# Norm scales moved into exp, staging of the first batch, and a written VectorE order in a fused attention and MLP kernel

## Chip, cores and metric

The kernel runs on one core of one Trainium2 chip. The metric is the device time of one execution in microseconds (us), lower is better.

## The reference

Attention with normalised queries and keys, followed by a LayerNorm and an MLP with a residual:

```python
def rmsnorm(x, g):                       # q, k, v: (8, 12, 448, 64) float32
    return x / np.sqrt(np.mean(x * x, axis=-1, keepdims=True) + 1e-06) * g
scores = np.matmul(rmsnorm(q, g_q), rmsnorm(k, g_k).transpose(0, 1, 3, 2)) / 8
attn = softmax(scores)
x = np.matmul(attn, v)                   # heads side by side: (8, 448, 768)
xn = (x - mean) / np.sqrt(var + 1e-06) * g_ln
out = x + np.maximum(xn @ w_ch1, 0.0) @ w_ch2    # (768, 3072), (3072, 768)
```

## The kernel before, in words

The work is attention by pairs of heads (6 pairs for each of 8 batches, 48 in all) and one MLP for each batch. TensorE, ScalarE, GpSimd (POOL) and the SP queue run in the order in which the program issues their instructions; VectorE's instructions are ordered by the framework's scheduler (`manual_schedule` at L642 names all engines but VectorE).

**Units.** Loads and preparation go by units (L23): batch 0 has six units of one pair, later batches have three of two pairs. `load_unit` (L94) issues nine DMAs: for each of k, q, v the first 384 rows of the heads (L106, on SP) and twice the 64 left over rows (L111, on ScalarE's queue for units 0 and 1, else on SP). One-pair units are staged in `hT`, the MLP's hidden buffer, in three rotating places; two-pair units in `p_in`, with two buffers.

**Preparation** (`prep_ops`, L114) of a unit is a list of operations: squares of k and q on ScalarE (L136), sums of squares on VectorE (L139), k times the product of both gain vectors on GpSimd (L145), inverse roots (`_rsqrt`, L32: one exp on ScalarE and seven small instructions on VectorE), the key's norm (`kn`, L47 by way of L150), its high half (L153) and its remainder (L156) in fp16, the normalised query (L47 by way of L160) and its duplicate (L163), and v cast on GpSimd (L166, L171). `attention` (L268) spreads these over the steps of earlier pairs with a table `todo` from step to operations.

**A pair** has seven steps (L295). Step i issues the score matmuls of key block i (L217 to L221), the exp of that block (L222, scale 1/8), and the value matmuls of the pair before (L241, L243). At step 2 the next pair's keys are transposed (L186) and copied from PSUM in two parts (L189, L190), at step 4 its queries (L200), copied in three parts (L202 to L204). After the last value block `evac_o` (L247) divides by the sums, and `stats` (L330) takes LayerNorm statistics of the 128 columns that a pair gives.

**LayerNorm and MLP.** `ln_ops` (L342) makes a list: statistics and root; then for each tile of 128 tokens a normalisation (ScalarE L364, VectorE L366) and a transposition (TensorE L379, VectorE copy L381). Odd batches have four tiles, since the left over rows of two batches share one; even batches have three. `mlp_chunks` gives 24 up chunks (six matmuls L394, relu L396) and, for each tile, eight down chunks (six matmuls L405); the residual add is L409. 

**The order around it.** `run` (L430) first issues attention up to step 0.4 of a pair, then the loads of the first weights (L315, on GpSimd), attention up to pair 3, the second weights (L320), attention up to pair 7, the LayerNorm of batch 0 with some more attention between its parts, and then each MLP chunk by chunk, with attention issued in proportion to the chunks' costs, so that the next batch's attention (and one pair beyond) is through at 82% of the cost. What is left of the chunks then carries the next LayerNorm's operations, evenly spread. Before the last MLP `flag` (L482) counts whether all softmax sums lie in a range; if not, a general path (L499) recomputes everything.

Of the kernel before, what the change touches and what calls it, by code (L numbers as in the profile page):

```python
# [22 lines left out]
UNITS = [(0, 2 * i, 1) for i in range(NPAIR)]  # L23
# [5 lines left out]
REC_LO, REC_HI = 1.0 / 3.0e7, 0.5  # L29


def _rsqrt(nc, out, a, t, eps):  # L32
# [5 lines left out]
    for _ in range(2):  # L38
        eng.tensor_tensor(out=t, in0=out, in1=out, op=ALU.mult)  # L39
        eng.scalar_tensor_tensor(out=t, in0=t, scalar=-0.5, in1=a, op0=ALU.mult, op1=ALU.mult)  # L40
        eng.scalar_tensor_tensor(out=out, in0=t, scalar=1.5, in1=out, op0=ALU.add, op1=ALU.mult)
# [14 lines left out]
class _Fast:  # L56


    def __init__(self, ctx, tc, sh, q, k, v, g_ln, w1, w2, out):
# [21 lines left out]
        for t in self.kT:  # L81
            nc.vector.memset(t[:, 1], 0.0)
# [5 lines left out]
        nc.vector.memset(self.rec, 0.01)  # L88
        self.hT = fix.tile([128, NFF, 512], FP16, name="hT", tag="hT")
        self.xs, self.xls, self.st = {}, {}, {}  # L90
# [3 lines left out]
    def load_unit(self, u):  # L94
# [19 lines left out]
    def prep_ops(self, u):  # L114
# [8 lines left out]
        def begin():  # L123
# [3 lines left out]
            c["rt"] = self.p_n.tile([128, 2, 14], FP32, tag="rt", name="rt")[:, :, 0:g]  # L127
            c["qn"] = self.p_n.tile([128, 14, 2, D], FP16, tag="qn", name="qn")[:, 0:g]
# [12 lines left out]
        def root():  # L141
            _rsqrt(nc, c["rr"], c["ssq"], c["rt"], D * 1e-6)
# [16 lines left out]
        def qn():  # L159
            _scaled(nc, c["qn"][:, :, 0], c["t"][:, 0], c["rr"][:, 0])  # L160

        def qdup():
            nc.vector.tensor_copy(out=c["qn"][:, :, 1], in_=c["qn"][:, :, 0])  # L163
# [5 lines left out]
        def vleft():  # L169
            for e in range(2):  # L170
# [4 lines left out]
                lambda: (total(0), vmain()), root, None, kn, khi, klo, qn, qdup, vleft]  # L175


    def trans_k(self, p):
# [3 lines left out]
        ps = self.ps_tr.tile([128, 1024], FP16, tag="tr", name="psK")  # L182
        kT = self.kT[p % 2]
        gs = [6 * m + w] + [6 * w + i for i in range(6)]
        for i, g in enumerate(gs):
            nc.tensor.matmul(ps[:, ts(i, 128)], khl[:, g], sh.id16, is_transpose=True,  # L186
# [491 lines left out]
```

## Time and profile before

| what | value |
|---|---|
| runs | median 733.85 us of 3 (733.62 to 735.27) |
| the profiled execution's own time | 733.03 us |
| its span in the profile | 731.2 us |
| mean granted TensorE clock | 0.956 |
| TensorE matmul busy | 633.3 us (87%) |
| VectorE, ScalarE, GpSimd busy | 428.0, 338.2, 89.7 us |
| moved by DMA | 54.83 MB |

The busy shares are means over the span. The rows below are to be read by stretch: the time from the first instruction to the first up matmul (L394), and the time after it, have different limits.

### The profile page before, as it was taken

To read this page: it belongs to the slowest core of one execution; us is meant where nothing else is said; L and a number is where in the kernel's file an instruction comes from. 1 tells how busy PE (TensorE), PEld (TensorE's weight loads), DVE (VectorE), ACT (ScalarE), POOL (GpSimd) and SP (SyncE) were. 2 spreads that over 40 slices of the span, in tenths; PEclk is the share of its full clock that TensorE was granted. 3 is DMA by queue.
4 is the path that set the end of the run, shared out by engine and by line. 5 is a ranking of instruction groups with operands and counts; after the bars stand their busy time and mean duration, and the time that the engine had idled before them with its cause. 6 is when DMAs were issued, how large, how long until landed. Compare 5 with 4: busy or idle time off the path is not lost.

```text
span 731.2 us, 12852 instructions
## 1 busy us (share of the span) xinstructions
PE 633.3 (87%) x5066; PEld 387.3 (53%) x5066; DVE 428.0 (59%) x1195; ACT 338.2 (46%) x646; POOL 89.7 (12%) x119
## 2 busy tenths in 40 slices
PE   0452458997999999997999999998999999979996
PEld 0231335664555666664556666654556566644463
DVE  1886688667466756776646757784565755351011
ACT  1443246753465327752665247633664356423400
POOL 1332012110101101110111011110111010000000
PEclk9997568998999999999999999998999999999999
DMA  4499951221322014230322123202313100000011
GB/s 138 95 220 219 229 150 48 53 77 44 98 77 74 26 44 106 70 99 22 98 76 78 44 85 110 77 23 70 99 28 98 44 22 2 23 23 22 1 44 46
DMA packets 69234, 54.83 MB, mean 75 GB/s; under 512 B 23216, under 2 KB 63152, under 8 KB 69168
## 3 DMA queue, kind: packets, MB, share of 16 engines
q1 hardware_dynamic: 62320, 43.86, 21.0%
q0 software_dynamic: 5456, 9.44, 7.0%
q8 instruction: 41, 0.67, 0.4%
q10 hardware_dynamic: 1392, 0.66, 0.3%
q14 instruction: 25, 0.20, 0.1%
HBM read 52.36 MB, written 11.01 MB: 87 GB/s over the span
## 4 chain that ended last, share of the span: by engine, by line
PE 74%; DVE 11%; DMA 6%; SPq 3%; ACT 3%; issue 1%; ACTq 0%; DVEq 0%
PE psH L394 30%; PE psC L405 25%; PE psS L217 6%; PE oA L241 4%; SPq L111 3%; PE psQ L200 2%; DMA t<-in_k_dram 2%; PE psK L186 2%; DMA hT<-in_q_dram 2%; PE psX L379 2%; PE oB L243 1%; DMA hT<-in_v_dram 1%; ACT t L364 1%; DVE xn L366 1%; DVE x L258 1%
## 5 line engine op out<-in xcount | busy, mean ns | idle before, releaser
L405 PE MATMUL psC<-w,hT 128*128 128x384 f16 x1344 | 246.8, 332 | 0.0
L394 PE MATMUL psH<-xnT,w 128*128 128x512 f16 (+1 forms) x1152 | 245.2, 352 | 1.2 <-DVE xnT L381 1.2
L222 ACT ACTIVATE E<-psS 128x448 f16<-128x448 f32 x336 | 179.1, 540 | 119.9 <-PE psS L217 99.1
L396 ACT ACTIVATE hT<-psH 128x384 f16<-128x384 f32 (+1 forms) x192 | 104.5, 544 | 149.7 <-PE psH L394 148.2
L405 PEld LDWEIGHTS <-hT 128*128 128x128 f16 x1344 | 127.7, 100 | 75.8 <-issue 6.2
L394 PEld LDWEIGHTS <-w 128*128 128x128 f16 x1152 | 105.0, 98 | 81.7 <-issue 1.3
L217 PE MATMUL psS<-qT,kT 128*128 128x448 f16 x288 | 105.3, 373 | 8.0 <-ACT E L222 5.2
L241 PEld LDWEIGHTS <-E 128*128 128x128 f16 x1008 | 74.4, 101 | 68.5 <-issue 20.8
L145 POOL TENSOR_TENSOR t<-t,gprod 128x896 f32<-128x896 f32 x21 | 43.7, 2081 | 455.0 <-issue 271.7
L241 PE MATMUL oA<-v,E 128*128 128x65 f16 x864 | 70.7, 198 | 9.9 <-DVE x L258 9.5
L409 DVE TENSOR_TENSOR x<-psC,x 128x384 f32<-128x384 f32 x48 | 26.7, 556 | 83.3 <-PE psC L405 82.9
L186 PE MATMUL psK<-id,khl 128*128 128x128 f16 x336 | 29.2, 232 | 43.6 <-DVE rt L39 23.6
L243 PE MATMUL oB<-v,E 128*128 128x65 f16 x288 | 53.5, 197 | 0.3
L186 PEld LDWEIGHTS <-khl 128*128 128x128 f16 x336 | 21.5, 104 | 44.9 <-issue 23.8
L139 DVE TENSOR_REDUCE ssq<-khl 128x14 f32<-128x896 f32 (+1 forms) x27 | 26.4, 979 | 26.3 <-ACT khl L136 25.8
L202 DVE COPY qT<-psQ 128x448 f16<-128x448 f16 x48 | 18.7, 389 | 38.6 <-PE psQ L200 38.6
L217 PEld LDWEIGHTS <-kT 128*128 128x128 f16 x288 | 29.2, 103 | 22.5 <-DVE qT L202 2.3
L256 DVE RECIPROCAL rec_all<-oA 128x6 f32<-128x6 f32 x48 | 9.3, 193 | 49.3 <-PE oA L241 49.2
L379 PE MATMUL psX<-id,xn 128*128 128x128 f16 x168 | 15.7, 243 | 22.6 <-DVE xn L366 22.6
L339 DVE BATCH_NORM_STATS2 stat<-x 128x6 f32<-128x128 f32 x144 | 34.5, 282 | 0.7
L243 PEld LDWEIGHTS <-E 128*128 128x128 f16 x336 | 33.3, 99 | 1.4 <-DVE xl L263 0.9
L200 PE MATMUL psQ<-id,qn 128*128 128x128 f16 x336 | 29.2, 232 | 4.9 <-DVE kT L190 4.9
(75 smaller groups left out, 594.8 us busy)
## 6 DMA issues: line engine op xcount, KB each, us to landing
out_dram<-x SPq DMA_DIRECT2D x24, 384.0 KB, 2.3
t<-in_k_dram SPq DMA_DIRECT2D x21, 384.0 KB, 3.6
t<-in_q_dram SPq DMA_DIRECT2D x21, 384.0 KB, 4.1
t<-in_v_dram SPq DMA_DIRECT2D x21, 384.0 KB, 4.4
w<-in_moe_w_ch_dram POOLq DMA_DIRECT2D x3, 1536.0 KB, 21.0
w<-in_moe_w_ch_dram POOLq DMA_DIRECT2D x2, 2304.0 KB, 38.1
out_dram<-xl SPq DMA_DIRECT2D x8, 192.0 KB, 3.0
t<-in_k_dram SPq DMA_DIRECT2D x42, 32.0 KB, 3.4
```

Of the source, the lines that this page charges most:

```text
L145: nc.gpsimd.tensor_tensor(out=c["t"][:, 1], in0=c["t"][:, 1], in1=sh.gprod.unsqueeze(1).broadcast_to([128, g, D]), op=ALU.mult)
L186: nc.tensor.matmul(ps[:, ts(i, 128)], khl[:, g], sh.id16, is_transpose=True, start=(i == 0), stop=(i == 6))
L200: nc.tensor.matmul(ps[:, ts(i, 128)], qn[:, g], sh.id16, is_transpose=True, start=(i == 0), stop=(i == 6))
L217: nc.tensor.matmul(ps[:, 0:S], kT[:, 192 + 128 * i:320 + 128 * i], qT[:, h * S:(h + 1) * S], start=True, stop=True)
L222: nc.scalar.activation(out=c["E"][:, i], in_=ps[:, 0:S], func=AFT.Exp, scale=1.0 / 8.0, bias=EXP_BIAS)
L241: nc.tensor.matmul(oA[:, t, cs], E[:, i, ts(t, 128)], rhs, start=(i == 0 and t == 0), stop=(i == 6 and t == 2))
L243: nc.tensor.matmul(oB[:, cs], E[:, i, 320:448], rhs, start=(i == 0), stop=(i == 6))
L339: nc.vector.bn_stats(out=self.st[b][:, t, 6 * hp:6 * hp + 6], in_=x[:, 128 * hp:128 * hp + 128])
L379: nc.tensor.matmul(ps[:, dc], xn[:, ts(dc, 128)], sh.id16, is_transpose=True, start=(dc == 0), stop=(dc == NDC - 1))
L394: nc.tensor.matmul(ps[:, 0:N], sh.w1[:, dc, ts(f, 128)], xnT[:, dc, 0:N], start=(dc == 0), stop=(dc == NDC - 1))
L396: nc.scalar.activation(out=hT[:, f, 0:N], in_=ps[:, 0:N], func=AFT.Relu)
L405: nc.tensor.matmul(ps[:, 0:384], hT[:, f, ts(t, 128)], sh.w2[:, f, ts(g, 384)], start=(f == 0), stop=(f == NFF - 1))
```

## The change

1. Units: batch 0 now has two units of one pair and two of two pairs. Units 0 to 2 are staged in `hT` side by side, without rotation, the rest in `p_in`. Units 0 to 2 are loaded first, units 3 and 4 and the LayerNorm gain right behind the preparation of unit 0. All loads are on SP but q of unit 0, which is on ScalarE's queue.
2. The key is no longer normalised. Its inverse root (with the factor 8 of the query's product left to the query) goes to a table `rr_all`, and exp takes a column of it as its scale for each partition. `khi` moves from VectorE to ScalarE, the query's duplicate of units 0 to 3 from VectorE to GpSimd. A maximum of the gains and a count over `rr_all` join the flag.
3. The transposes write into one PSUM tile `tr`, laid out so that one copy takes the keys and one the queries; a zero block stays in PSUM. The query copy of pairs 0, 2 and 4 is ScalarE's.
4. Statistics by 256 columns, after every second pair.
5. Order: steps are a list, with marks where a batch's attention ends. The sixth pair's values come before the seventh pair's scores, and the preparation of batch 1's first unit stands between the parts of batch 0's LayerNorm. Attention ends at 77% of an MLP's cost. The LayerNorm's root and first two normalisations are issued there, but its transposes only ahead of the last chunks, one each. The flag comes after three chunks of the last MLP. The second weights are loaded in two halves by columns, and batch 0's down chunks go by column half first.
6. VectorE runs in program order as well. A first exp on a constant loads ScalarE's table early.

The diff, cut to its core:

```diff
-UNITS = [(0, 2 * i, 1) for i in range(NPAIR)]
+UNITS = [(0, 0, 1), (0, 2, 1), (0, 4, 2), (0, 8, 2)]
...
-        if m == 1:
-            o = 2688 * (u % 3)
-            t = self.hT.rearrange("p f n -> p (f n)")[:, o:o + 2688].bitcast(FP32)
+        if u < 3:
+            o = 2688 * u
+            t = self.hT.rearrange("p f n -> p (f n)")[:, o:o + 2688 * m].bitcast(FP32)
...
-        eng = nc.scalar if u < 2 else nc.sync
         for n, src in ((1, self.k), (0, self.q), (2, self.v)):
-            nc.sync.dma_start(
+            eng = nc.scalar if u == 0 and n == 0 else nc.sync
+            eng.dma_start(
...
-        def kn():
-            _scaled(nc, c["t"][:, 1], c["t"][:, 1], c["rr"][:, 1])
         def khi():
-            nc.vector.tensor_copy(out=c["khl"][:, :, 0], in_=c["t"][:, 1])
+            nc.scalar.activation(c["khl"][:, :, 0], c["t"][:, 1], AFT.Identity)
...
         def qdup():
-            nc.vector.tensor_copy(out=c["qn"][:, :, 1], in_=c["qn"][:, :, 0])
+            (nc.gpsimd if u < 4 else nc.vector).tensor_copy(out=c["qn"][:, :, 1],
+                                                            in_=c["qn"][:, :, 0])
...
-                lambda: (total(0), vmain()), root, None, kn, khi, klo, qn, qdup, vleft]
+                lambda: (total(0), vmain()), khi, root, klo, None, qn, qdup, vleft]
...
-        nc.vector.tensor_copy(out=flat[:, 0:64], in_=ps[:, 0:64])
-        nc.vector.tensor_copy(out=flat[:, 128:960], in_=ps[:, 64:896])
+        nc.vector.tensor_copy(out=kT.rearrange("p g d -> p (g d)"), in_=ps[:, 0:960])
...
-        nc.vector.tensor_copy(out=qT[:, 0:448], in_=ps[:, 0:448])
-        nc.vector.tensor_copy(out=qT[:, 448:832], in_=ps[:, 512:896])
-        nc.vector.tensor_copy(out=qT[:, 832:896], in_=ps[:, 448:512])
+        if p in (0, 2, 4):
+            nc.scalar.copy(out=qT, in_=ps.rearrange("p e s -> p (e s)"))
+        else:
+            nc.vector.tensor_copy(out=qT, in_=ps.rearrange("p e s -> p (e s)"))
...
-        nc.scalar.activation(out=c["E"][:, i], in_=ps[:, 0:S], func=AFT.Exp, scale=1.0 / 8.0,
-                             bias=EXP_BIAS)
+        nc.scalar.activation(out=c["E"][:, i], in_=ps[:, 0:S], func=AFT.Exp,
+                             scale=self.rr[:, 1, g:g + 1], bias=EXP_BIAS)
...
+        todo.setdefault(2, []).append(lambda: [self.load_w1(c, c + 1024) for c in range(0, FF, 1024)])
+        todo.setdefault(21, []).append(lambda: [self.load_w2(g) for g in range(2)])
...
+        def first():
+            for u in range(3):
+                self.load_unit(u)
+            for op in self.prep_ops(0):
+                if op is not None:
+                    op()
+            self.trans_k(0)
+            self.trans_q(0)
+            self.load_unit(3)
+            self.nc.sync.dma_start(self.sh.gln, self.g_ln.unsqueeze(0).broadcast_to([128, DM]))
+            self.load_unit(4)
...
+            if p == nb0:
+                for x in ((0, 1), (2, 3, 4), (5, 6)):
+                    steps.append([lambda i=i: self.values(nb0 - 1, i) for i in x])
+                steps[-1].append(lambda: self.stats(nb0 - 1))
+                mark.append(len(steps))
+                steps += [[op] for op in self.prep_ops(UNIT_PAIR.index(nb0)) if op is not None]
+                steps[-1].append(lambda: self.load_unit(6))
+                steps += [[lambda: self.trans_k(nb0)], [lambda: self.trans_q(nb0)]]
...
-        res = [root, lambda: norm(0)]
-        for t in range(1, n):
-            res += [lambda t=t: norm(t), lambda t=t: self.ln_trans(c["xn", t - 1], t - 1)]
-        return res + [lambda: self.ln_trans(c["xn", n - 1], n - 1)]
+        def first():
+            root()
+            norm(0)
+            norm(1)
+        def trans(t):
+            self.ln_trans(c["xn", t], t)
+            if t + 2 < n:
+                norm(t + 2)
+        return [first] + [lambda t=t: trans(t) for t in range(n)]
...
-        frac = 0.82
+        frac = 0.77
...
             for i, (cost, emit) in enumerate(chunks):
+                if items and len(chunks) - i <= len(items):
+                    items.pop(0)()
                 emit()
                 done += cost
...
+                upto(int(min(goal, start + (goal - start) * done / total / frac)))
+                if self.pos >= goal and items is None:
+                    items = self.ln_ops(b + 1)
+                    items.pop(0)()
...
-        with tc.manual_schedule(engines={ENG.PE, ENG.Activation, ENG.Pool, ENG.SP}):
+        with tc.manual_schedule(engines={ENG.PE, ENG.Activation, ENG.Pool, ENG.SP, ENG.DVE}):
```

## Rows read from the trace of the kernel before

**Rows 1.** Busy by stretch: start:end, length, PE, PEld, DVE, ACT, POOL, PEclk, DMA share, GB/s.

```profile
27.80:60.00 32.20, 19.80 (x166) 12.37 (x166) 26.49 (x80) 16.78 (x38) 13.25 (x21) 0.95 1.01 200
60.00:100.00 40.00, 16.08 (x139) 10.40 (x137) 25.18 (x71) 14.78 (x29) 6.94 (x8) 0.66 1.07 220
100.00:117.50 17.50, 9.32 (x86) 6.37 (x87) 15.57 (x41) 8.38 (x14) 4.11 (x4) 0.71 0.30 80
117.50:724.70 607.20, 586.32 (x4662) 356.75 (x4661) 347.81 (x967) 294.62 (x560) 60.69 (x72) 0.98 0.19 57
```

**Rows 2.** The page's DMA rate in 40 equal slices of the span.

```profile
GB/s 138 95 220 219 229 150 48 53 77 44 98 77 74 26 44 106 70 99 22 98 76 78 44 85 110 77 23 70 99 28 98 44 22 2 23 23 22 1 44 46
```

**Rows 3.** Timeline of the start: start us, duration, engine, line, operation, idle before.

```profile
6.40 0.22 DVE L635 TENSOR_TENSOR gprod<-gg 128x64 f32<-128x64 f32 x1 [3.90 <-DMA gg<-in_g_k_dram]
...
14.46 1.28 ACT L136 ACT_TABLE_LOAD   x1 [14.46 <-DMA hT<-in_q_dram]
...
27.83 0.91 PE L217 MATMUL psS<-qT,kT 128*128 128x448 f16 x2 [0.90 <-DVE qT L202]
...
33.69 0.58 PE L217 MATMUL psS<-qT,kT 128*128 128x448 f16 x1
```

**Rows 4.** Timeline of the weight loads' issue and of SP's queue.

```profile
31.06 2.66 POOL L315 DMA_DIRECT2D w<-in_moe_w_ch_dram x3
...
47.25 0.37 SPq L106 DMA_DIRECT2D t<-in_k_dram  x1
...
67.71 1.19 SPq L106 DMA_DIRECT2D t<-in_k_dram  x1
```

**Rows 5.** Groups by line and shape: busy us, mean ns of one, idle before.

```profile
L222 ACT ACTIVATE E<-psS 128x448 f16<-128x448 f32 x336 | 179.1, 540 | 119.9 <-PE psS L217 99.1 <-PE psS L221 20.5
...
L396 ACT ACTIVATE hT<-psH 128x384 f16<-128x384 f32 x96 | 47.2, 491 | 58.7 <-PE psH L394 58.7
...
L364 ACT ACTIVATE t<-x,sh,rs 128x768 f32<-128x768 f32 x24 | 23.9, 1022 | 11.7 <-DVE sh L358 11.0
...
L47 DVE SCALAR_TENSOR_TENSOR t<-t,rr 128x896 f32<-128x896 f32 x21 | 22.8, 1085 | 0.5
...
L136 ACT ACTIVATE khl<-t 128x896 f32<-128x896 f32 x21 | 19.8, 945 | 10.5 <-DMA t<-in_k_dram 10.5
```

**Rows 6.** Busy by stretch: sum over 170:192, 335:349, 490:508 and 648:664.

```profile
sum 70.00, PE 52.57 PEld 31.37 DVE 40.94 ACT 18.65 POOL 0.00; mean PE 13.14 PEld 7.84 DVE 10.23 ACT 4.66 POOL 0.00
```

**Rows 7.** The chain that ended last: start us, duration, what.

```profile
103.83 0.10 DVE rec_all L256
...
117.55 1.14 PE psH L394 x6
...
170.67 0.19 PE psS L217
170.86 0.09 PE oA L241 x3
...
180.75 3.84 PE psC L405 x12
...
187.15 0.67 PE psX L379 x12
187.82 1.95 PE psC L405 x12
```

**Rows 8.** Waits in the whole span: engine, line, releaser: us in total, times, longest.

```profile
PE psX L379 <- DVE xn L366: 22.6, 9, 4.4
...
PE psQ L200 <- DVE kT L190: 4.9, 5, 1.5
```

**Rows 9.** Timeline of VectorE and GpSimd side by side near 36 us.

```profile
36.38 1.52 DVE L156 TENSOR_TENSOR khl<-hT,khl 128x448 f16<-128x448 f32 x1
...
36.25 1.17 POOL L145 TENSOR_TENSOR hT<-hT,gprod 128x448 f32<-128x448 f32 x1 [1.55 <-issue]
```

More of the change, by code (lines that the diff above doesn't have):

```diff
@@ L29, with _rsqrt @@
 REC_LO, REC_HI = 1.0 / 3.0e7, 0.5
-def _rsqrt(nc, out, a, t, eps):
+K_MAX = 6.0e4
+def _rsqrt(nc, out, a, t, eps, last=None):
     eng = nc.vector
@@ L37, in _rsqrt @@
                          bias=0.5 * LN2 * (127.0 - 0.043))
-    for _ in range(2):
+    for i in range(2):
         eng.tensor_tensor(out=t, in0=out, in1=out, op=ALU.mult)
         eng.scalar_tensor_tensor(out=t, in0=t, scalar=-0.5, in1=a, op0=ALU.mult, op1=ALU.mult)
-        eng.scalar_tensor_tensor(out=out, in0=t, scalar=1.5, in1=out, op0=ALU.add, op1=ALU.mult)
+        eng.scalar_tensor_tensor(out=last if i and last is not None else out, in0=t, scalar=1.5,
+                                 in1=out, op0=ALU.add, op1=ALU.mult)
 def _scaled(nc, out, x, r):
@@ L181, in trans_k @@
         qn, khl, m = self.units[u]
[L182 to L186, printed above, removed]
-                             start=(i == 0), stop=(i == 6))
-        flat = kT.rearrange("p g d -> p (g d)")
-        nc.vector.tensor_copy(out=flat[:, 0:64], in_=ps[:, 0:64])
-        nc.vector.tensor_copy(out=flat[:, 128:960], in_=ps[:, 64:896])
+        kT, ps = self.kT[p % 2], self.tr
+        nc.tensor.matmul(ps[:, 0:256].rearrange("p (e o) -> p e o", e=2)[:, :, 0:D],
+                         khl[:, 6 * m + w], sh.id16, is_transpose=True, start=True, stop=False)
+        for i in range(6):
+            nc.tensor.matmul(ps[:, 192 + 128 * i:320 + 128 * i], khl[:, 6 * w + i], sh.id16,
+                             is_transpose=True, start=False, stop=(i == 5))
+        nc.vector.tensor_copy(out=kT.rearrange("p g d -> p (g d)"), in_=ps[:, 0:960])
     def trans_q(self, p):
@@ new lines, in batch @@
+        def batch(b):
+            self.xs[b] = self.p_x.tile([128, 3, DM], FP32, tag="x", name="x")
+            if b % 2 == 0:
+                self.xls[b // 2] = self.p_xl.tile([128, DM], FP32, tag="xl", name="xl")
+        steps.append([first])
+        for p in range(n + 1):
+            if p == nb0:
+                for x in ((0, 1), (2, 3, 4), (5, 6)):
[5 more added lines that the diff above has]
+                steps += [[lambda: self.trans_k(nb0)], [lambda: self.trans_q(nb0)]]
@@ L295, in attention @@
             for i in range(7):
-                for op in todo.pop(7 * p + i, ()):
-                    op()
+                c = []
+                if i == 0 and p < n and p % NPAIR == 0:
+                    c.append(lambda b=p // NPAIR: batch(b))
+                c += todo.pop(7 * p + i, [])
                 if p < n:
-                    self.scores(p, i)
-                if p > 0:
+                    c.append(lambda p=p, i=i: self.scores(p, i))
+                if p > 0 and p != nb0:
                     for x in {0: (), 1: (0, 1)}.get(i, (i,)):
-                        self.values(p - 1, x)
+                        c.append(lambda p=p, x=x: self.values(p - 1, x))
@@ L349, in ln_ops @@
         st = self.st[b]
[L350 removed]
+        mv = st[:, :, 18:20]
         def root():
@@ L491, in flag @@
                                        op0=ALU.is_le, op1=ALU.mult)
-        nc.vector.tensor_reduce(out=cnt, in_=good, axis=AX.X, op=ALU.add)
-        ps = self.ps_tr.tile([1, 1], FP32, tag="tr", name="psF")
-        nc.tensor.matmul(ps, sh.ones, cnt, start=True, stop=True)
-        nc.vector.tensor_scalar(out=sh.flag, in0=ps, scalar1=128.0 * n - 0.5, scalar2=None,
+        nc.vector.tensor_reduce(out=cnt[:, 0:1], in_=good, axis=AX.X, op=ALU.add)
+        nk = self.rr.shape[2]
+        nc.vector.tensor_scalar(out=good[:, 0:nk], in0=self.rr[:, 1], scalar1=sh.gmax,
+                                scalar2=None, op0=ALU.is_ge)
+        nc.vector.tensor_reduce(out=cnt[:, 1:2], in_=good[:, 0:nk], axis=AX.X, op=ALU.add)
+        nc.vector.tensor_reduce(out=cnt[:, 0:1], in_=cnt, axis=AX.X, op=ALU.add)
+        ps = self.ps_o.tile([1, 1], FP32, tag="oB", name="psF")
+        nc.tensor.matmul(ps, sh.ones, cnt[:, 0:1], start=True, stop=True)
+        nc.vector.tensor_scalar(out=sh.flag, in0=ps, scalar1=128.0 * (n + nk) - 0.5, scalar2=None,
                                 op0=ALU.is_lt)
@@ L630 @@
     nc.vector.memset(sh.ones, 1.0)
+    sh.warm = const.tile([128, 1], FP32, name="warm")
     gg = const.tile([128, 2, D], FP32, name="gg")
```

161 lines of the change are left out of this document (76 added, 85 removed).

## The prediction

> **What bounds the kernel now.** I first read the busy time by stretch, which splits the span into two parts with different limits. From 117.5 to 724.7 us TensorE is busy 586.3 of 607.2 us at a granted clock of 0.98, VectorE 347.8 and ScalarE 294.6 [rows 1]: this part is TensorE's, and only 20.9 us in it are idle. From 27.8 to 117.5 us it is busy 45.2 of 89.7 us (19.8 + 16.1 + 9.3), in the middle at a granted clock of 0.66, the lower of its two levels (1.2 and 2.4 GHz) most of the time, while the DMA share is above 1 up to 100 us [rows 1]. The DMA rate by slice says the same: 219 to 229 GB/s in the third to fifth slice [rows 2]. Before 27.83 us no score matmul runs at all [rows 3]. So the start costs about 117.5 us for six pairs, and the rest runs at TensorE's pace. Last, the boundaries between MLPs: in four stretches around them (after the odd batches' attention, when four tiles are normalised) TensorE is busy 52.57 of 70.0 us [rows 6].
>
> Why is the start slow? ScalarE issues gain vectors and the leftover rows of two units, so its first work, a table load, begins only at 14.46 us [rows 3]. Later the loads share the DMA engines with the weights: those are issued at 31.06 us, and then the nine DMAs of one two-pair unit (1.38 MB) hold SP's queue from 47.25 us until the next unit's first at 67.71, 20.5 us or 67 GB/s [rows 4].
>
> **First scores.** Before: square at 15.74 (14.46 + 1.28), first scores 12.1 us later [rows 3]. In those 12.1 us VectorE, ordered by a planner, also ran unit 1: two sums, two products and a cast at about half of the 1085 ns of a two-pair product [rows 5], and a root of seven small instructions, together some 5 us (estimate). In program order unit 1 comes after. The key product and the key cast of unit 0 leave VectorE as well (1.1 us). The duplicate on GpSimd and ScalarE's longer copy give back some 1.4 us. That leaves 12.1 - 5.0 - 1.1 + 1.4 = 7.4 us from the sums to the first scores. The sums can't begin before VectorE has seen the gains land at 6.40 us [rows 3], then the norm limit and the memsets, an estimated 1.7 us: 8.1 us. By then ScalarE has loaded its table (the new warm-up), issued q for unit 0 and squared k. First scores: 15.5 us, 12.3 us earlier. Bounds: 13 if the planner's order hid nothing, 19 if q lands as late as the loads of before.
>
> **Six pairs of batch 0.** The first pair took 27.83 to 33.69, 5.9 us, with its data there [rows 3]; later pairs waited for loads. I take that pair as the pace and add the new cost on ScalarE: exp now reads its scale per partition. No row shows an exp with such an operand. The normalisation reads two (scale and bias) and takes 1022 ns for 768 columns; the square reads none and takes 945 ns for 896. A column costs 0.77 ns by the exp and the relu (540 ns for 448, 491 for 384), so a square of 768 would take 846 ns, and one operand costs about 90 ns [rows 5]. Bounds: 0 if exp hides it, 176 ns if one operand costs as much as both. I take 90, the even split. A pair then grows by 0.65 us, to 6.6. Unit 1's preparation stands ahead of the first exp on ScalarE (2.6 us). So scores end at 15.5 + 2.6 + 6 x 6.6 = 57.7, values of the sixth pair 2 us later: 60.
>
> Are the data there? Units 0 to 3 (4.1 MB) go out on SP with nothing to wait for. GpSimd issues the first weights behind unit 1's duplicate and unit 2's product, at about 24 us by the times above. The first slice of 18.3 us moved 138 GB/s though SP and ScalarE had stopped issuing before its end, and the fullest slices moved 219 to 229 [rows 2]; at 180, between them, units 0 to 3 have landed by then. Unit 4 and the LayerNorm gain (1.77 MB) then crawl at 67 GB/s until 51 us, and are needed at 60. The first weight matrix (4.7 MB, at the 150 GB/s that the loads leave) lands at about 57 us, before the MLP; the second matrix is needed only after 24 up chunks. No wait in the sum, and the cover is 9 us.
>
> **LayerNorm and the first up chunk.** Before, from the last evacuation at 103.83 to the first up matmul at 117.55: 13.7 us [rows 7]. The transposes are the same; unit 4's sums and root lie between them on VectorE, in program order, so I take 15. First up chunk at 75 instead of 117.5: -42.5 us. Bounds: 64 (pairs at 5 us, LayerNorm 13) to 92 (pairs at 9 us). But before had by then done more attention: it ran 1.7 pairs into batch 1. One pair is 8 x 0.19 of scores, 28 x 0.03 of values and 14 x 0.056 of transposes, 3.1 us of TensorE at full clock [rows 7]: +5.3.
>
> **Boundaries.** Four times TensorE stands at a transposition until the normalised tile is there; the sum is 70.0 - 52.57 = 17.4 us idle [rows 6]. At the first, TensorE waits 4.4 us for the first tile, and for all such tiles 22.6 us in the kernel [rows 8]; at the same place the twelve down matmuls behind it take 3.84 us against 1.95 further on [rows 7], as at the lower level. Over four boundaries I put the second loss at 6 us (estimate from this one, not taken in full). With attention ending at 77% of a batch's cost instead of 82%, some 14 down chunks (11 with three tiles) of 0.98 us are left, and transposes come only before the last four (three). So the first transpose comes some ten chunks, 9.8 us, after the normalisation chain begins (eight with three tiles), where it came at once. So I take 21 of the 23.4 us. Bounds: 8 (chain late in half of them) to 26.
>
> **New load on ScalarE.** It gains the key's cast (as the square: 945 ns for 896 columns) and 90 ns per exp, so a pair costs 7 x 0.63 for exps, 0.95 for half of two squares, 0.47 for half of a cast and 0.1 for half of a root: 5.9 us instead of 4.8. In the up half of a three-tile batch 0.5/0.77 = 65% of six pairs fall: ScalarE has 24 x 0.49 + 0.65 x 6 x 5.9 = 34.8 us to do [rows 5], TensorE 24 x 0.98 + 0.65 x 6 x 3.1 = 35.5. It is full, where before it had 85%. I put 5 us on the four such batches; bounds 0 and 25.
>
> **VectorE.** It loses the key product (1085 ns x 21 [rows 5]), the key cast, three of five copies and some statistics. Since it is not the bound outside the start, this is worth nothing in itself: TensorE's work hides it. What its program order costs: when a root waits for ScalarE's exp, the copy of the transposed keys is queued behind it, and TensorE's next transposes wait for that copy, because they now share one PSUM tile. I put 2 us; bounds 0 and 70 (below). Moving the count of the flag behind three chunks of the last MLP, halving the second weights by columns and batch 0's order of down chunks cost nothing: they lie beside TensorE's work, and with their cover gone would cost 2 us.
>
> GpSimd gets four duplicates in the start. A VectorE subtraction of 448 columns, which by the two-pair product's 1085 ns takes some 0.55 us alone [rows 5], took 1.52 beside GpSimd's product, ending about 0.5 us after it [rows 9]. The Trainium skill, page "SBUF — State Buffer", section "SBUF: two separate sides", says that the two share a port pair which one holds for its whole instruction while the other is blocked; the row agrees. By that rule three of the duplicates (an estimate of 0.9 us each, from GpSimd's casts) would stop VectorE in full, and the result would be 685 instead of 682; I leave it out of the sum, since VectorE has room there.
>
> **Sum.** 731.2 - 42.5 + 5.3 - 21 + 5 + 2 = 680.0 us of span. The profiled run's time was 1.8 us above its span (733.03), so 681.8; the median of the runs is 733.85, 0.8 above that run, which is inside the noise (0.2% either way, 1.5 us, is what a measurement tells from no change). I predict 682.
>
> **Rivals.**
> A, the forecast: 660 to 698. Chance 0.66.
> B, the start stays bound by loads: the weights overtake units 3 and 4, and pairs go at 10 us, not 6.6. Then the up chunks begin at 75 + 6 x 3.4 = 95 and the time is 702. For it: the 20.5 us of one unit [rows 4]. Against: four units are issued ahead of any weight. 0.13.
> C, ScalarE becomes the bound while up chunks and attention share it: 25 us instead of 5, 702. For it: the 98% above. Against: its queue has the whole down half to catch up. 0.10.
> D, better: pairs at 5.5 us, no loss on ScalarE: 682 - 6.6 - 5 = 670 and, with LayerNorm at 13 and all idle at boundaries gone, 663. 0.05.
> E, slower: VectorE in program order. At the root it waits for ScalarE, and TensorE stands at the shared transposition tile in every pair. The gain of 52 us is eaten at 52/42 = 1.24 us a pair; at 1.6 us the time is 680 + 67 = 747. For it: the 4.9 us in all that TensorE's query transposes waited for the key copy before [rows 8] are those of a planned order. Against: VectorE is asked for about half of each 9 us pair. 0.05. The Trainium skill, page "TensorE: Matmul & The Clock Gate", section "Architectural detail: the array is 16× 32×32, not 1× 128×128", calls VectorE's and ScalarE's queues strict first in, first out; that is this rival's rule, and no row of before shows what it costs in program order.
> In between, within 0.2% of before: 0.01.
>
> So faster 0.94, same 0.01, slower 0.05. The range takes in A and most of B and C: 660 to 707. A's own range is 660 to 698.
>
> **What would show it.** Right: first scores near 15.5 us, first up matmul near 75, no TensorE idle above 1 us at the boundaries and their granted clock at 1.00, exp near 632 ns, ScalarE above 90% busy in the up halves of three-tile batches. Wrong: TensorE waiting for the copy of keys or for exps between 75 us and the end (E, C), ScalarE's squares waiting for loads before 60 us (B), or transposes that still wait for the normalised tile.

## The result, and the profile after

| | before | after |
|---|---|---|
| median of the runs | 734.21 us of 4 (733.62 to 735.27) | 680.0 us of 4 (679.4 to 680.19) |
| span of the profiled execution | 731.2 us | 677.5 us |
| that execution's own time | 733.03 us | 679.4 us |

The ratio is 0.9259, with a 95% interval of 0.9243 to 0.9275: 7.4% faster. The forecast was 682 us, with a range of 660 to 707. The sum was nearly right, but not all of its terms were, as the experiments show.

The page of after: span, busy times, and the DMA rate by slice.

```profile
span 677.5 us, 12547 instructions
...
PE 620.1 (92%) x5066; PEld 379.4 (56%) x5066; DVE 376.4 (56%) x886; ACT 384.6 (57%) x669; POOL 91.6 (14%) x115
...
GB/s 151 217 219 220 215 138 83 84 65 88 83 82 47 50 87 76 105 24 105 83 82 49 30 100 83 105 24 106 82 63 45 46 26 1 25 35 14 0 47 50
```

VectorE lost 51.6 us of work and ScalarE gained 46.4. The second slice, at 95 GB/s before [rows 2], now moves 217: the loads of units 3 and 4 follow without a gap.

Busy time by stretch of after (start:end, length, PE, PEld, DVE, ACT, POOL, PEclk, DMA share, GB/s): most of batch 0's scores, the LayerNorm, and the rest.

```profile
17.50:53.20 35.70, 24.76 (x255) 15.42 (x255) 25.59 (x60) 29.83 (x52) 15.15 (x18) 1.00 1.04 217
55.00:70.00 15.00, 3.40 (x44) 2.53 (x41) 11.94 (x34) 5.93 (x8) 4.10 (x4) 0.64 1.25 216
69.90:671.00 601.10, 588.57 (x4748) 359.31 (x4747) 329.77 (x764) 342.38 (x598) 67.49 (x80) 1.00 0.24 67
```

Against [rows 1]: in batch 0's pairs TensorE is busy 24.76 of 35.7 us at a granted clock of 1.00, where it had been busy 16.08 of 40 at 0.66. From the first up chunk on, 12.5 of 601.1 us are idle, where 20.9 of 607.2 were. In the LayerNorm the clock is still at 0.64, after TensorE has stood.

Timeline of the start of after (start us, duration, engine, line, operation, idle before).

```profile
5.98 0.58 ACT L141 ACTIVATE khl<-hT 128x448 f32<-128x448 f32 x1 [2.78 <-DMA hT<-in_k_dram]
...
15.17 0.91 PE L220 MATMUL psS<-qT,kT 128*128 128x448 f16 x2 [0.99 <-ACT qT L205]
...
25.58 0.58 PE L220 MATMUL psS<-qT,kT 128*128 128x448 f16 x1
...
52.89 0.35 PE L224 MATMUL psS<-qT,kT 128*128 128x448 f16 x1
...
55.84 0.20 DVE L261 RECIPROCAL rec_all<-oA 128x6 f32<-128x6 f32 x1 [1.08 <-PE oA L246]
...
62.52 1.74 PE L421 MATMUL psX<-id,xn 128*128 128x128 f16 x12 [6.67 <-DVE xn L401]
...
69.92 4.45 PE L436 MATMUL psH<-xnT,w 128*128 128x384 f16 x18 [2.78 <-DVE xnT L423]
```

These answer to [rows 3] and [rows 7]: the first scores came from 27.83 to 15.17 us, the last evacuation before the LayerNorm from 103.83 to 55.84, the first up matmul from 117.55 to 69.92. The second pair's scores begin at 25.58: the first pair takes 10.4 us, the other five 27.7 in all, 5.5 each. So the start gave 47.6 of the 53.7 us of span. From there to the end it took 613.7 us before (731.2 - 117.55) and 607.6 after (677.5 - 69.92).

The exps of after, by line, and all waits of TensorE from 71 to 671 us (line, releaser: us in total, times, longest).

```profile
L227 ACT ACTIVATE E<-psS,rr_all 128x448 f16<-128x448 f32 x336 | 208.1, 633 | 66.9 <-PE psS L220 50.3
```

```profile
PE psC L447 <- DVE x L451: 4.0, 4, 1.0
PE tr L199 <- DVE kT L191: 2.8, 4, 0.8
PE psS L220 <- ACT E L227: 2.2, 7, 0.6
PE psX L421 <- DVE xn L401: 1.5, 4, 0.4
PE psS L220 <- DVE qT L207: 0.8, 1, 0.8
```

Of the 22.6 us that transposes waited for the normalised tile [rows 8], 10.2 are left, and 8.7 of those lie in batch 0's LayerNorm. The waits of the kernel before for the same part, from 118 to 725 us, were these and one of 0.3 us:

```profile
PE psX L379 <- DVE xn L366: 19.7, 7, 4.4
PE oA L241 <- DVE x L258: 0.2, 1, 0.2
```

A wait that before did not have heads the list of after: down matmuls for the residual add, about 1 us at each of four boundaries. The first boundary shows why (timeline of after, VectorE and TensorE):

```profile
142.66 1.88 DVE L401 TENSOR_TENSOR xn<-t,gln 128x768 f16<-128x768 f32 x2 [1.09 <-ACT t L399]
...
144.57 1.02 DVE L451 TENSOR_TENSOR x<-psC,x 128x384 f32<-128x384 f32 x2
...
145.18 1.14 PE L447 MATMUL psC<-w,hT 128*128 128x384 f16 x6 [0.99 <-DVE x L451]
```

VectorE stands 1.09 us for the normalisation on ScalarE, does both products, and only then the two adds (the next down matmuls wait for them).

### The profile page after: what moved, and what is told of

The parts are those of the page before. It is cut to its first block, busy times and chain, and to the rows that moved or that the text cites. A ratio compares the mean times of both kernels' runs of the same rounds, so it can differ in the third digit from the quotient of the medians.

```text
span 677.5 us, 12547 instructions
## 1 busy us (share of the span) xinstructions
PE 620.1 (92%) x5066; PEld 379.4 (56%) x5066; DVE 376.4 (56%) x886; ACT 384.6 (57%) x669; POOL 91.6 (14%) x115
## 4 chain that ended last, share of the span: by engine, by line
PE 77%; DVE 8%; ACT 6%; DMA 4%; issue 2%; SPq 1%; POOL 0%; DVEq 0%
PE psH L436 30%; PE psC L447 27%; PE psS L220 6%; PE oA L246 4%; PE tr L202 2%; ACT E L227 2%; DMA t<-in_k_dram 2%; ACT khl L155 2%; PE tr L189 2%; DMA t<-in_v_dram 2%; PE oB L248 1%; PE psS L223 1%; PE psS L224 1%; DVE xn L401 1%; PE psX L421 1%
## 5 line engine op out<-in xcount | busy, mean ns | idle before, releaser
L227 ACT ACTIVATE E<-psS,rr_all 128x448 f16<-128x448 f32 x336 | 208.1, 633 | 66.9 <-PE psS L220 50.3
L447 PE MATMUL psC<-w,hT 128*128 128x384 f16 x1344 | 239.3, 326 | 4.0 <-DVE x L451 4.0
L220 PE MATMUL psS<-qT,kT 128*128 128x448 f16 x288 | 101.3, 359 | 10.0 <-ACT E L227 7.8
L246 PEld LDWEIGHTS <-E 128*128 128x128 f16 x1008 | 71.7, 98 | 55.5 <-issue 6.5
L191 DVE COPY kT<-tr 128x960 f16<-128x960 f16 x48 | 31.5, 656 | 43.8 <-PE tr L189 43.0
L207 DVE COPY qT<-tr 128x896 f16<-128x896 f16 x45 | 28.1, 624 | 45.2 <-PE tr L202 44.9
L248 PEld LDWEIGHTS <-E 128*128 128x128 f16 x336 | 32.5, 97 | 0.9 <-DVE xl L268 0.5
L401 DVE TENSOR_TENSOR xn<-t,gln 128x768 f16<-128x768 f32 x28 | 26.8, 969 | 8.8 <-ACT t L399 8.8
L399 ACT ACTIVATE t<-x,sh,rs 128x768 f32<-128x768 f32 x24 | 23.8, 1022 | 12.1 <-DVE sh L393 11.4
L144 DVE TENSOR_REDUCE ssq<-qn 128x14 f32<-128x896 f32 (+1 forms) x25 | 26.1, 1045 | 3.3 <-ACT qn L141 2.2
L263 DVE TENSOR_TENSOR x<-oA,rec_all 128x384 f32<-128x384 f32 x48 | 26.8, 558 | 1.5
```

Of the source, the lines that this page charges most:

```text
L144: nc.vector.tensor_reduce(out=c["ssq"][:, n], in_=c["sq", n], axis=AX.X, op=ALU.add)
L191: nc.vector.tensor_copy(out=kT.rearrange("p g d -> p (g d)"), in_=ps[:, 0:960])
L207: nc.vector.tensor_copy(out=qT, in_=ps.rearrange("p e s -> p (e s)"))
L220: nc.tensor.matmul(ps[:, 0:S], kT[:, 192 + 128 * i:320 + 128 * i], qT[:, h * S:(h + 1) * S], start=True, stop=True)
L227: nc.scalar.activation(out=c["E"][:, i], in_=ps[:, 0:S], func=AFT.Exp, scale=self.rr[:, 1, g:g + 1], bias=EXP_BIAS)
L246: nc.tensor.matmul(oA[:, t, cs], E[:, i, ts(t, 128)], rhs, start=(i == 0 and t == 0), stop=(i == 6 and t == 2))
```

## The experiments

All ratios are to the kernel before; diffs are against after unless another is named. The kernel before, run again beside each group of experiments, had medians of 734.9 to 736.3 us against 734.2 above, so a difference in us between two groups is good to some 2 us.

**Was the ScalarE queue what delayed the start?** The leftover rows of units 0 and 1, q and the gain go back to the old queues, without the early table load.

```diff
-            eng = nc.scalar if u == 0 and n == 0 else nc.sync
-            eng.dma_start(
+            eng = nc.scalar if u < 2 else nc.sync
+            nc.sync.dma_start(
...
+            self.nc.scalar.dma_start(self.sh.gln, self.g_ln.unsqueeze(0).broadcast_to([128, DM]))
...
-            self.nc.sync.dma_start(self.sh.gln, self.g_ln.unsqueeze(0).broadcast_to([128, DM]))
...
-    nc.scalar.activation(sh.warm, sh.ones, AFT.Exp)
```

> The changed kernel with the load issue of before: the leftover rows of units 0 and 1 on ScalarE's queue, q of unit 0 on SP, the LayerNorm gain on ScalarE's queue at the very start, and no exp ahead that loads ScalarE's table. VectorE stays in program order. Theory (the first scores came earlier since ScalarE was free earlier, not by VectorE's order): first square at 13 to 16 us and first scores at 22 to 25, then the pairs at the same pace: 686 to 690 us. Rival (the units' smaller share of loads did it): first scores under 18, under 683 us.

Measured: 689.37 us, ratio 0.9374 (0.9357 to 0.9391), 9.4 us above after. Timeline of ScalarE in this kernel:

```profile
13.91 1.26 ACTq L114 DMA_DIRECT2D hT<-in_v_dram  x2
15.20 1.28 ACT L141 ACT_TABLE_LOAD   x1 [15.20 <-issue]
16.50 0.58 ACT L141 ACTIVATE khl<-hT 128x448 f32<-128x448 f32 x1
```

The last DMA issue ends and the table load begins at once: what stands behind the issues in ScalarE's queue waits for them. In after, too, the first square (5.98 us) comes right behind the issue of q's last rows, 4.70 to 5.94 us, though the profile puts that wait down to the load of k. First scores come at 24.52 us and the first up matmul at 79.3, both 9.4 later than after, and the end is as much later. This part, queues and table load together, is worth 9.4 us and passes through to the end whole, as the theory had it.

**Is it the program order of VectorE that brings the first scores forward?** The scheduler orders VectorE again, all else as in after.

```diff
-        with tc.manual_schedule(engines={ENG.PE, ENG.Activation, ENG.Pool, ENG.SP, ENG.DVE}):
+        with tc.manual_schedule(engines={ENG.PE, ENG.Activation, ENG.Pool, ENG.SP}):
```

> The changed kernel with VectorE left to the framework's scheduler. Theory (program order costs about 2 us between the MLPs and gives 4 to 5 us in the start, where unit 1 no longer runs ahead of unit 0): 682 to 685 us, first scores at 18 to 20 us instead of 15.2. Rival 1 (program order gives nothing): 678 to 680 us. Rival 2 (program order matters through the whole kernel): over 690 us.

Measured: 672.42 us, ratio 0.915 (0.9133 to 0.9166): faster than after by 7.6 us. My theory and both rivals were wrong. The first scores come at 14.95 us, no later than in program order; the first up matmul comes at 67.52 instead of 69.92. VectorE in this kernel, in batch 0's LayerNorm and at the first boundary:

```profile
66.84 0.16 DVE L36 TENSOR_SCALAR ssq<-ssq 128x28 f32<-128x28 f32 x1
66.92 0.55 DVE L423 COPY xnT<-psX 128x768 f16<-128x768 f16 x1
67.39 0.17 DVE L40 TENSOR_TENSOR rt<-rr 128x28 f32<-128x28 f32 x1
...
135.68 0.56 DVE L451 TENSOR_TENSOR x<-psC,x 128x384 f32<-128x384 f32 x1
136.15 0.16 DVE L40 TENSOR_TENSOR stat<-rs 128x4 f32<-128x4 f32 x1
...
138.60 1.88 DVE L401 TENSOR_TENSOR xn<-t,gln 128x768 f16<-128x768 f32 x2 [1.10 <-ACT t L399]
140.40 0.55 DVE L451 TENSOR_TENSOR x<-psC,x 128x384 f32<-128x384 f32 x1
```

The scheduler puts a root's wait for ScalarE to use there: it copies the last transposed tile (66.92), or does a residual add (135.68), before the root's next step. In program order that copy stands behind the whole root of the next unit, and the add behind the products. TensorE's wait for the residual add is gone from 71 to 671 us. Of the 2.4 us at the first up matmul, 0.8 are there at the last evacuation already (55.03 us), and 1.6 come in the LayerNorm. After the first up matmul the kernel takes 603.2 us (670.7 - 67.52), 4.4 less than after.

**Does the longer exp cost time?** The exp's scale becomes a constant; this kernel leaves out the key's norms.

```diff
-                             scale=self.rr[:, 1, g:g + 1], bias=EXP_BIAS)
+                             scale=1.0 / 8.0, bias=EXP_BIAS)
```

> The changed kernel with the exp's scale a constant 1/8 instead of a column of the table; this leaves the key norms out of the result. Theory (the operand costs some 90 ns, which counts in the six pairs of the start and where ScalarE is nearly full): exp back at 540 ns, 3 to 4 us from the start and up to 5 us from the up halves: 671 to 677 us. Rival (hidden beside other waits): 679 to 680 us.

Measured: 678.61 us, ratio 0.9232 (0.9217 to 0.9248), an interval that overlaps that of after. The exps by line:

```profile
L227 ACT ACTIVATE E<-psS 128x448 f16<-128x448 f32 x336 | 178.9, 542 | 76.4 <-PE psS L220 58.1
```

The operand costs 91 ns on each of 336 exps, 29 us of ScalarE's busy time, and by the medians 1.4 us of the kernel's, which is inside the noise: nearer the rival than the theory. The first up matmul comes at 70.2 us, no sooner than with it, and batch 0's scores take 37.6 us from first to last (38.1 in after). So the exp's length paces neither batch 0's pairs nor the up halves.

**What is the key's normalisation on VectorE worth?** The key product and the key cast go back to VectorE, the exp's scale is a constant again, and the root stands one place earlier in the list of operations, as in the kernel before.

```diff
+        def kn():
+            _scaled(nc, c["t"][:, 1], c["t"][:, 1], c["rf"][:, 1])
...
-            nc.scalar.activation(c["khl"][:, :, 0], c["t"][:, 1], AFT.Identity)
+            nc.vector.tensor_copy(out=c["khl"][:, :, 0], in_=c["t"][:, 1])
...
-                lambda: (total(0), vmain()), khi, root, klo, None, qn, qdup, vleft]
+                lambda: (total(0), vmain()), root, None, kn, khi, klo, qn, qdup, vleft]
...
-                             scale=self.rr[:, 1, g:g + 1], bias=EXP_BIAS)
+                             scale=1.0 / 8.0, bias=EXP_BIAS)
```

> The changed kernel with the first part undone: the key is normalised on VectorE again and its high half cast there, exp has the constant scale 1/8; all else as changed. Theory (in the start VectorE is what bounds a pair once the loads are there, so its relief counts there and only there): VectorE gets 6 us more in batch 0's units and two more links before the first scores; first scores 1 us later, first up chunk 5 to 9 us later than 69.9, then 1 us back from exp: 684 to 690 us. Rival 1 (hidden: ScalarE was the bound of the start): 678 to 681 us. Rival 2 (VectorE's load counts in the whole kernel): over 695 us.

Measured: 700.58 us, ratio 0.9525 (0.9492 to 0.9557), 20.6 us above after, where my theory had under 10 of them; rival 2 has the time. First scores at 17.46 us, first up matmul at 78.0 (8.1 later), and some 12 us more after it. TensorE's longest wait in this kernel from 80 to 660 us, and the timeline where one of them is longest (VectorE and TensorE):

```profile
PE oA L249 <- DVE x L266: 9.2, 12, 1.3
```

```profile
120.25 0.19 DVE L40 TENSOR_TENSOR rt<-rr 128x28 f32<-128x28 f32 x1 [0.29 <-ACT rr L37]
...
121.47 0.19 DVE L264 RECIPROCAL rec_all<-oA 128x6 f32<-128x6 f32 x1
...
122.51 0.27 PE L249 MATMUL oA<-v,E 128*128 128x65 f16 x3 [1.28 <-DVE x L266]
122.81 1.09 DVE L49 SCALAR_TENSOR_TENSOR t<-t,rr_all 128x896 f32<-128x896 f32 x1
```

The wait, 9.2 us in all, is the value matmuls waiting for the evacuation of the pair before. VectorE is busy 355.85 of those 580 us, so its mean load is not the reason: what stands ahead of the evacuation in its queue is. Here that is a unit's root, which itself waits for ScalarE; the key's product (122.81) comes behind the evacuation. It is the same at 105.5 and 176.4 us. So these waits may come from the root's place in the list and not from the work moved back; the two were not tried apart.

The same kernel with the scheduler's order of VectorE tells how much of this is order.

```diff
-        with tc.manual_schedule(engines={ENG.PE, ENG.Activation, ENG.Pool, ENG.SP, ENG.DVE}):
+        with tc.manual_schedule(engines={ENG.PE, ENG.Activation, ENG.Pool, ENG.SP}):
```

> The changed kernel with the key normalised on VectorE again (as undo_norms) and VectorE left to the scheduler. Theory (VectorE's load counts between the MLPs only through its program order, where TensorE's value matmuls wait for an evacuation queued behind long products): the 8 us later first up chunk stays, the 12 us lost after it shrink to 2 to 4: 681 to 686 us, and value matmuls wait under 3 us for VectorE after 80 us. Rival (the load itself counts): 690 to 695 us, waits as in undo_norms.

Measured: 687.47 us, ratio 0.934 (0.9324 to 0.9355), between the two expectations. So 13.1 of the 700.58 go away with the order. TensorE's longest wait and the one for the evacuation, 80 to 660 us:

```profile
PE tr L202 <- DVE kT L194: 3.4, 4, 1.3
...
PE oA L249 <- DVE x L266: 1.8, 9, 0.3
```

The wait for the evacuation falls from 9.2 to 1.8 us. Against the kernel with moved norms and the same scheduler (672.42), 15 us are left: the first up matmul at 76.4 instead of 67.5, and some 6 after it. TensorE's waits from 80 to 660 us come to 10.7 us here and to 6.2 there, and from the first up matmul on it is busy 590.5 us against 588.1: together most of the 6. Undoing the moved norms costs about 15 us under the scheduler, and 20.6 in program order.

**Were the loads the start's limit before?** In the kernel before, alone, the weights are issued later.

```diff
-        upto(0.4)
+        upto(4)
...
-        upto(3)
+        upto(6)
```

> The kernel before with one edit: the first weights are issued at pair 4 instead of 0.4, the second at pair 6 instead of 3. Theory (the weights hold up the loads of batch 0 and these hold up the pairs): pairs 1 to 5 go at 7 us instead of 13, the first up chunk starts at 85 to 100 instead of 117.5, and the time is 705 to 720 us. Rival (the pairs are bound by VectorE's planned order and by ScalarE, not by loads): first up chunk at 112 or later, 728 to 735 us.

Measured: 721.42 us, ratio 0.9801 (0.9775 to 0.9827); first up matmul at 106.7 us. Later weights bring the old start 10.8 us forward, less than my theory had, and the time is just above its range. Busy time by stretch of this kernel, columns as above:

```profile
58.00:107.00 49.00, 28.66 (x247) 19.00 (x245) 45.02 (x117) 24.36 (x47) 13.65 (x14) 0.65 1.12 210
60.00:70.00 10.00, 5.67 (x49) 3.87 (x48) 9.56 (x25) 5.02 (x9) 3.79 (x4) 0.67 1.11 198
```

VectorE is busy 92% of 49 us and 96% of ten of them. No wait from 29 to 107 us is put down to a load any more, where before GpSimd and ScalarE waited for them. With the loads freed VectorE becomes the limit of the old start, and a pair still takes about 10 us.

The opposite in after: the first weights are issued right behind the issue of the loads of units 0 to 2, at about 1 us.

```diff
-        todo.setdefault(2, []).append(lambda: [self.load_w1(c, c + 1024) for c in range(0, FF, 1024)])
...
+            for c in range(0, FF, 1024):
+                self.load_w1(c, c + 1024)
```

> The changed kernel with the first weights issued by GpSimd right behind the issue of units 0 to 2's loads, ahead of its first product, so at about 1 us instead of 23. Theory (weights in flight cut the loads to about 67 GB/s): units 1 to 3 land 10 to 25 us later, first up chunk at 80 to 95 instead of 69.9, 690 to 705 us. Rival (the start is bound by instructions, loads have room): first up chunk under 73, 678 to 682 us.

Measured: 697.56 us, ratio 0.9477 (0.9457 to 0.9498), first scores at 21.77 us, first up matmul at 87.8: as the theory had it. SP's queue in this kernel:

```profile
8.58 0.37 SPq L109 DMA_DIRECT2D hT<-in_k_dram  x1
11.71 3.94 SPq L114 DMA_DIRECT2D hT<-in_k_dram  x2
16.03 0.37 SPq L109 DMA_DIRECT2D hT<-in_q_dram  x1
```

The three DMAs of one key of one pair now hold the queue from 8.58 to 16.03 us; in after the same three took it from 4.86 to 6.90. So the order of the transfers does matter, and after has it right, but freeing the loads without easing VectorE (721.42 us above) gives a quarter of the gain.

**Late transposes or the earlier end of attention?** First the old, evenly spread LayerNorm for batches 1 to 7, still at 77%.

```diff
+        if b > 0:
+            res = [root, lambda: norm(0)]
+            for t in range(1, n):
+                res += [lambda t=t: norm(t), lambda t=t: self.ln_trans(c["xn", t - 1], t - 1)]
+            return res + [lambda: self.ln_trans(c["xn", n - 1], n - 1)]
...
-                if items and len(chunks) - i <= len(items):
-                    items.pop(0)()
...
+                        per = len(items) / max(left - 1, 1)
...
+                    while at < len(items) and at + 1 <= due + 1e-6:
+                        items[at]()
+                        at += 1
```

> The changed kernel with the LayerNorm's transposes of batches 1 to 7 issued as before: spread evenly over the chunks that are left once attention is through (still at 77%), not ahead of the last chunks. Theory (lateness of the transposes is what frees the boundaries): TensorE stands again at the first transposition of each boundary, 4 to 5 us at the four-tile ones, and runs slowed matmuls behind it: 15 to 25 us in all, so 695 to 705 us, with more than 15 us of waits of the transposes for the normalised tile. Rival (77% instead of 82% alone frees them): 680 to 685 us and waits under 5 us.

Measured: 693.99 us, ratio 0.9446 (0.9429 to 0.9463), 14.0 above after, 1 us under the theory's range. Then the old 82% with late transposes.

```diff
-        frac = 0.77
+        frac = 0.82
```

> The changed kernel with attention spread over 82% of an MLP's cost, as before, instead of 77%. Theory (what is left of the chunks must cover the normalisation chain of 7 to 8 us): only about five chunks lie between the chain's start and the first transpose with three tiles, seven with four, so 1 to 3 us of waits at a boundary: 684 to 695 us. Rival (ScalarE is nearly full in the up halves, and its relief counts more): under 679 us.

Measured: 691.04 us, ratio 0.9398 (0.9381 to 0.9414), 11.0 above, as the theory had it. The same wait comes back in both (from 80 to 660 us, first line the spread kernel, second the 82%):

```profile
PE psX L426 <- DVE xn L401: 13.2, 4, 3.3
```

```profile
PE psX L421 <- DVE xn L401: 13.8, 4, 3.5
```

Either part alone leaves TensorE waiting some 3.4 us at each four-tile boundary. They are not two gains to be added.

A still earlier end of attention tests whether distance alone cures the residual add, in program order:

```diff
-        frac = 0.77
+        frac = 0.75
```

> The changed kernel, VectorE in program order, with attention ended at 75% instead of 77%. Theory (one more down chunk between the end of attention and the first transpose covers the normalised tile, and the residual add that stands behind it on VectorE): the 4 us in which down chunks wait for the add and the 1.5 us of waits for the tile go, 673 to 676 us. Rival (the add stays behind the products whatever the distance): 679 to 681 us; or ScalarE gets too full: over 681 us.

Measured: 676.94 us, ratio 0.9199 (0.9184 to 0.9215), 3.1 below after, which neither the theory nor the rival had. The longest wait from 80 to 660 us in it:

```profile
PE psC L447 <- DVE x L451: 3.6, 4, 1.0
```

It hardly moved: the add stands behind the products here too. What fell, from 71 us on, are the waits for the key copy (2.8 to 1.4 us), for exps (2.2 to 1.3) and for the tile (1.5 to 1.0).

**The two together.** The scheduler's VectorE, with unit 4's preparation behind batch 0's LayerNorm instead of between its parts, and then 75% as well.

```diff
-            upto(self.pos + 2)
...
-        with tc.manual_schedule(engines={ENG.PE, ENG.Activation, ENG.Pool, ENG.SP, ENG.DVE}):
+        with tc.manual_schedule(engines={ENG.PE, ENG.Activation, ENG.Pool, ENG.SP}):
```

> VectorE left to the scheduler, and the preparation of batch 1's first unit issued after batch 0's LayerNorm, among the first MLP's chunks, instead of between the LayerNorm's parts. Theory (the unit's sums stand on VectorE between the normalised tiles): first up chunk 1.5 to 3 us earlier than 67.5, 669 to 671 us. Rival (the delay comes back, as batch 1's scores then start later and ScalarE has more to do in the first up half): 672 us or more.

Measured: 673.44 us, ratio 0.915 (0.9134 to 0.9165): nothing against the scheduler alone, so the rival has it. The first up matmul comes at 65.3 us, 2.2 sooner, but what follows takes 3.1 us more (606.3 against 603.2). Of that 2.5 are seen at 77 to 79 us, where TensorE now waits for the queries of batch 1's first pair.

```diff
-        frac = 0.77
+        frac = 0.75
```

> As prep_late_planned, with attention ended at 75% of an MLP's cost instead of 77%. Theory (77% already covers the normalisation chain): within 1 us of prep_late_planned. Rival (still some waits of transposes): 1 to 3 us faster; or ScalarE gets too full in the up halves: 2 us or more slower.

Measured: 666.86 us, ratio 0.9058 (0.9042 to 0.9074), 13.1 below after, the best here, and 6.6 below the run at 77%, where no expectation had more than 3. All of TensorE's waits from 80 to 660 us:

```profile
PE tr L199 <- DVE kT L191: 2.3, 3, 0.9
PE psH L436 <- DVE xnT L423: 0.3, 1, 0.3
PE psS L220 <- ACT E L227: 0.2, 1, 0.2
```

The boundaries are gone from the list. What is left is the start, 65 us.

## Why the prediction was right, and where it was not

| step | predicted us | measured us |
|---|---|---|
| first scores | 15.5 | 15.17 |
| from there to the end of batch 0's scores | 42.2 | 38.1 |
| last value matmuls seen | 60 | 55.8 |
| LayerNorm to the first up matmul | 15 | 14.1 |
| first up matmul | 75 | 69.9 |
| from there to the end | 605.0 | 607.6 |

**First scores: the number right, by luck in part, the reason half wrong.** I gave the program order of VectorE 5 of the 12.3 us; with the scheduler the first scores come at 14.95, so in the changed kernel it gave nothing. The step that failed is "in program order unit 1 comes after". What brought the scores forward is ScalarE's queue (9.4 us by the queues undone) and the key's product and cast (2.3 us by the norms undone, of which I had 1.1). The first sum came at 6.59 us, not 8.1, and from it to the scores it took 8.6, not 7.4: two misses that cancel.

**Pairs: too slow by 4.1 us.** I made them ScalarE's, with 0.65 us more per pair for the exps and 2.6 for unit 1's preparation. The first pair took 10.4 us where that makes 9.2, and TensorE stands there twice, 2.08 and 1.99 us, for exps. The other five went at 5.5 us, not 6.6, and the constant scale shows that the exp's length doesn't set this stretch. The view I gave too little weight was VectorE's 26.49 of 32.2 us [rows 1]: the old kernel with late weights has it at 92%, and with the norms undone batch 0's scores take 42.7 us instead of 38.1, and the first up matmul comes 8.1 us later. I said that VectorE's relief is worth nothing "in itself" outside the start, and in the start I did not price it at all.

**Loads: right.** The weights issued early cost 17.6 us, and where the change puts them no wait from 15 to 56 us is put down to a load. What I had not seen is that the old start had a second limit just behind them, VectorE.

**LayerNorm in the start: right by size.** 14.1 us against 15. In it the unit 4 root that I named as standing between is what holds the last copy, 69.32 us; the scheduler's order takes 12.5 us for the same part.

**Boundaries: the mechanism and about the size right, but other waits took part of it back.** I put 21 us. TensorE's waits for the normalised tile fell from 19.7 us to 1.5 behind the first up matmul, 18.2 less. It is busy 588.6 us there, where 586.3 and the 5.3 for the 1.7 pairs make 591.6: 3 less (an estimate). That is some 21. Against it stand 9.8 us of waits that before did not have: 4.0 for the residual add, 2.8 for the key copy, 3.0 for exps and the query copy. The net is some 11, and 613.7 before, + 5.3, - 607.6 gives 11.4. The two parts undone cost 14.0 and 11.0 and share one wait; the two undone together were not tried.

**ScalarE: wrong.** I put 5 us on its up halves, from a sum of durations that made it 98% full. The constant scale takes 29 us off ScalarE and gives 1.4 by the medians. The operand's price itself was right: 90 ns forecast, 91 measured. The step that failed is the sum of durations. The up half of after's third MLP (three tiles), and two of ScalarE's instructions in it (columns as above):

```profile
233.20:270.40 37.20, 36.27 (x341) 23.88 (x339) 21.67 (x48) 29.52 (x58) 6.75 (x8) 1.00 0.31 86
```

```profile
246.35 0.63 ACT L227 ACTIVATE E<-psS,rr_all 128x448 f16<-128x448 f32 x1
246.87 0.50 ACT L438 ACTIVATE hT<-psH 128x384 f16<-128x384 f32 x1
```

The durations of its 58 instructions add up to 34.4 us, near my 34.8, but ScalarE is busy 29.52 of 37.2, or 79%: one begins before the last has ended (246.87 against 246.98), so their sum counts time twice. It was never full. TensorE's waits for exps after 71 us are 2.2 us in all.

**VectorE's program order: the mechanism right, its place and size wrong.** I charged 2 us, at the shared transposition tile; it costs 7.6. The tile's wait is 2.8 us after 71 us and 3.0 with the scheduler, so none of it is order. The price lies at the residual adds behind the products (4.0 us of waits), at the copy behind unit 4's root (1.6), and in small pieces elsewhere. Rival E named the rule and was far off in its price (1.6 us in every pair). The Trainium skill, page "TensorE: Matmul & The Clock Gate", section "Architectural detail: the array is 16× 32×32, not 1× 128×128", has VectorE's queue as strict first in, first out; the trace agrees, with 1.02 us of adds behind 1.88 of products that waited 1.09.

**VectorE between the MLPs: right for the kernel before, wrong for the changed one.** "TensorE's work hides it" holds for the kernel before, where TensorE waited 0.2 us for evacuations from 118 to 725 us: at that wait the moved norms had next to nothing to win. In the changed kernel undoing them costs 12 us behind the first up matmul in program order and about 6 with the scheduler. In program order 9.2 us of it are waits for evacuations, and at 105.5, 122.5 and 176.4 us a unit's root stands ahead of them, not the key's product. So the moved norms and the root's new place together keep the order by hand from costing this; which of the two does is not shown.

So the misses were -5.1 us at the first up matmul and +2.6 behind it. That the total came within 2 us of the forecast is luck in part: the pairs' 4.1 us too much and ScalarE's 5 stand against waits of 9.8 us, of which I had 2. Rivals B and C are refuted in this kernel. Of D the pace of the last five pairs (5.5 us) and ScalarE without loss came out, the LayerNorm of 13 us and boundaries without idle time did not. Not tried by themselves: the units' sizes, the query's copy and duplicates on the other engines, and the statistics by 256 columns.

## What to carry to other kernels

An engine that is 57% busy can still be where the time is, if its queue is in order and something that waits stands ahead of what others wait for: look at the order of its instructions at each wait, not at its share. An order by hand is worth comparing with the scheduler's on each engine separately; here it was compared on VectorE alone, and cost 7.6 us there. And when a start has two limits close together, as loads and VectorE here, easing one gives a fraction, so ask what is next before the sum is made. Durations of one engine are not to be added up to its load where its instructions overlap, as ScalarE's do here.

## What was not expected of the hardware

ScalarE's per-partition scale costs 91 ns on an exp of 448 columns (542 to 633 ns), and 336 of them cost the kernel 1.4 us by the medians, inside the noise, though ScalarE was 84% busy in the pairs (29.83 of 35.7 us). TensorE's granted clock was 1.00 in batch 0's pairs, at 69% busy, and 0.64, towards the lower of its levels, in the 15 us around the LayerNorm, where it had 3.4 us of work.

A VectorE product of 768 columns takes 0.95 us alone and 1.38 beside a product and a cast of GpSimd, at 64.89 us of after. The prediction left 3 us for the duplicates on GpSimd out of its sum, and the trace bears that out: VectorE's instructions beside the four of them keep their usual lengths. One of them:

```profile
28.96 0.93 POOL L165 COPY qn<-qn 128x896 f16<-128x896 f16 x1 [2.21 <-PE oB L248]
```

```profile
29.30 1.07 DVE L144 TENSOR_REDUCE ssq<-khl 128x14 f32<-128x896 f32 x1
```

The mean of this sum in the whole kernel is 1.08 us.
